# First-load order, fused low parts, single storage of rounded keys and queries, and a later fourth-pair load in an adaLN transformer block

## The chip, the cores and the metric

The kernel runs on one core of one Trainium2 chip. The metric is device microseconds of that core. TensorE (PE) does matmuls and transposes through an identity matrix, VectorE (DVE) and ScalarE (ACT) do elementwise work and read PSUM, GpSimd (POOL) does elementwise work in SBUF, and SyncE (SP) issues nearly all DMAs; in the changed kernel one DMA is issued by ACT.

## The reference

One transformer block over S = 2048 tokens of width D = 512, with 32 heads of width 16 and a hidden width F = 1792, all in float32. Six modulation vectors come from one conditioning row c.

```python
mod = (silu(c) @ w_mod)                      # c: 1 x 512, w_mod: 512 x 3072
sa, ca, ga, sb, cb, gb = six slices of 512
h = layernorm(x) * (1 + ca) + sa
q, k, v = h @ wqkv                           # 32 heads of 16
x = x + ga * (softmax(q k^T / 4) v @ wo)
h = layernorm(x) * (1 + cb) + sb
x = x + gb * (mish(h @ w1 + b1) @ w2)
```

## The kernel before

Every large product is made of three products of parts. A value is rounded to a high part (`hi_copy`) and its remainder is the low part (`lo_sub`), and high by high, high by low and low by high are summed in PSUM (`mm3`). `h_h` and `h_l` are the two parts of h, `wh` and `wl` those of a slice of wqkv, `qh` and `ql` those of the keys or queries just made.

**First stage.** Four blocks of 512 tokens (`tb` = 0 to 3), each of four tiles `xt`. For a block: row statistics on DVE (`stats_tb`, BN_STATS and BN_AGGR), the inverse square root on POOL (`ln_rs`), the normalisation on ACT (`apply_tb`), PE transposes (`tr_tb`), then per 128 channels `h_h` on ACT, `hf` on DVE (the same value unrounded) and `h_l` = `hf` - `h_h`, on DVE for the channels that `LOV[tb]` lists and on POOL for the others. `modc` holds 1 + ca and sa as columns, so nothing of h can be made before the conditioning row has gone through silu (`sil`), the products with `wma` (the two slices of w_mod), and back into columns. In block 0 DVE takes the statistics of block 1 before its first `hf`. After each block's matmuls the keys of the first eight heads (in block 0 the queries too) go to DRAM (`kscr`, `qscr`) and come back as operands with one head per 64 partitions.

**Operands of the scores.** A buffer `qa` or `ka` holds a pair of heads. `ka` has 48 rows per head (high, low, high of each of 16 dimensions), `qa` has 50 (high, high, low, and two rows for the row maximum, `mt`), so that one matmul sums all three products. Before the change `kscr` has 48 rows and `qscr` 50 rows per head, with the high parts stored twice. `load_pair` loads pair `pp` into one of five buffer pairs (`NR`).

**Steps.** From there on work is written out by hand in steps: 20 prologue steps (`PRO`) that take only the row maxima of the first heads (`max_pair`, L553 and L555) beside the remaining projections (`whole_units`), then T = 512 steps. Sixteen steps serve one group of four heads (one `n`): scores (L588), exponential (L591), product with the values (L606), and maxima for the group after next (L539, L541). `neg_max` (L562) closes the maxima of a group and PE goes on with the next group's first pair; eight steps later it needs the second pair. Each step has two hooks, numbered 2t and 2t+1, at which loads and stores are issued: `load_v` of group n at hook 32n - 11, the even pair of group n at 32(n-2) plus 2, 9 or 15, the odd pair at 32(n-1), the maxima's rows (`qa<-mt`) at 32n - 6. The fourth pair (pp = 3) of the first loads has a hook of its own. SP takes its DMAs strictly in that order, and the program gives them eight completion counters in turn, so an issue waits for the DMA eight before it.

The projection for the other query blocks and the MLP of finished blocks run inside these steps; a tail does the last block's MLP.

Of the kernel before, what the change touches and what calls it, by code (L numbers as in the profile page):

```python
# [8 lines left out]
F32 = mybir.dt.float32  # L9
# [9 lines left out]
def adaln_block(ctx: ExitStack, tc: tile.TileContext, x, wqkv, wo, w1, b1, w2, c, w_mod, out):  # L19
# [21 lines left out]
    LOV = ((1,), (), (1, 3), (1, 3))  # L41
# [10 lines left out]
    nc.scalar.preload_act_table_set("natural_log_exp_and_others")  # L52
# [4 lines left out]
    kscr = dram.tile([H, 48, S], F32, name="kscr")  # L57
    qscr = dram.tile([H, 50, S], F32, name="qscr")
# [16 lines left out]
    sel = cst.tile([P, 1], F32, name="sel")  # L75
    nc.gpsimd.memset(sel, 0.0)
    for k in range(DK):
        nc.gpsimd.memset(sel[32 * k:32 * k + 1, :], 1.0)
# [89 lines left out]
    def free_banks():  # L168
# [3 lines left out]
        for i in nc.cur_bb.bb.instructions:  # L172
            banks, names, made = set(), set(), set()
            for a in (*i.outs, *i.ins):
                v = getattr(a, "bass_ap", None)
                if v is not None and v.tensor.name != ring_t.tensor.name:
                    names.add(v.tensor.name)
                    if any(a is w for w in i.outs):
                        made.add(v.tensor.name)
# [66 lines left out]
    def qk_unit(kind, ct, tb, tag):  # L246
# [7 lines left out]
        def fin(h=None):  # L254
# [10 lines left out]
            scr, rows = (qscr, 50) if kind == 0 else (kscr, 48)  # L265

            def put():
                put_away.add((kind, ct, tb))
                o = 8 * ct * rows * S + tb * TB
                if kind == 0:  # L270
                    for r, src in enumerate((qh, qh, ql)):
                        nc.sync.dma_start(dap(scr, o + r * S, [[rows * S, 8], [3 * S, DH], [1, TB]]), src.bitcast(F32))
# [33 lines left out]
    def load_q(pp, rows=50):  # L306
# [5 lines left out]
        for s in range(2):  # L312
            nc.sync.dma_start(qt[64 * s:64 * s + rows, :], qscr[h + s, :rows, qb * TB:(qb + 1) * TB])

    def load_k(pp, tb=None):
# [3 lines left out]
        at_ = slice(0, S) if tb is None else slice(tb * TB, (tb + 1) * TB)  # L319
        assert {(1, h // 8, i) for i in (range(NB) if tb is None else (tb,))} <= put_away, (pp, put_away)  # L320
        for s in range(2):
            nc.sync.dma_start(kt[64 * s:64 * s + 48, at_], kscr[h + s, :, at_])
# [6 lines left out]
    with ExitStack() as es:  # L329
        lp = es.enter_context(tc.tile_pool(name="lp", bufs=1))  # L330
        cc = lp.tile([P, DK], F32, name="cc")
        nc.sync.dma_start(cc, c.rearrange("o (k p) -> p (o k)", p=P))
# [31 lines left out]
        nc.vector.tensor_mul(sil, cc, e)  # L364

# [21 lines left out]
        def first_norm():  # L387

            mv = lp.tile([P, 4, 2], F32, tag="ln_mv4", name="ln_mv4", bufs=2)
            rs = lp.tile([P, 4, 4], F32, tag="ln_rs4", name="ln_rs4", bufs=3)  # L390
            for h in range(2):
                two = slice(2 * h, 2 * h + 2)
                for i in range(2 * h, 2 * h + 2):
                    st_ = lp.tile([P, 6], F32, tag="ln_st", name="ln_st", bufs=4)
                    nc.vector.bn_stats(out=st_, in_=xts[i])
                    nc.vector.bn_aggr(out=mv[:, i, :], in_=st_)
                nc.gpsimd.tensor_scalar(rs[:, 0, two], mv[:, two, 1], 1.0, EPS, op0=ALU.mult, op1=ALU.add)
                nc.gpsimd.tensor_scalar(rs[:, 3, two], mv[:, two, 0], -1.0, 0.0, op0=ALU.mult, op1=ALU.add)
                nc.gpsimd.tensor_tensor(rs[:, 1, two], rs[:, 0, two], nhalf.to_broadcast([P, 2]), op=ALU.pow)
                nc.gpsimd.tensor_mul(rs[:, 2, two], rs[:, 3, two], rs[:, 1, two])  # L400
                if h == 0:
                    hi_k = split_hi(1, 0)
            return rs, hi_k

        def split_hi(kind, i, eng="p"):
# [4 lines left out]
        def split_lo(kind, i, hi):  # L410
            lo = lp.tile([P, DK, P], F32R, tag="wl", name="wl", bufs=2)
            lo_sub("p", lo, slices[kind, i], hi)
            slices[kind, i] = (hi, lo)

        def first_apply(rs, i, eng):
            xt = xts[i]
            if eng == "a":
                nc.scalar.activation(xt, xt, AF.Identity, scale=rs[:, 1, i:i + 1], bias=rs[:, 2, i:i + 1])
            else:
                nc.vector.tensor_scalar(xt, xt, rs[:, 1, i:i + 1], rs[:, 2, i:i + 1], op0=ALU.mult, op1=ALU.add)  # L420

        def first_tr():
            pts = [bank(("ring", "ms", "ring", "acc")[k]) for k in range(DK)]
            for ii in ((0,), (1,), (2, 3)):
                for k in range(DK):
                    for i in ii:
                        nc.tensor.transpose(pts[k][:, i * P:(i + 1) * P], xts[i][:, k * P:(k + 1) * P], ident)
            return pts

        def tr_tb(tb, ks=range(DK), pts=None):  # L430
            for k in ks:
# [9 lines left out]
                nc.vector.tensor_scalar(hf, pt, modc[:, 1, k:k + 1], modc[:, 0, k:k + 1], op0=ALU.mult, op1=ALU.add)  # L441
                lo_sub("v" if k in LOV[tb] else "p", h_l[:, k, s], hf, h_h[:, k, s])

        rs, hi_k = first_norm()
        pr, pm = [], bank()[:, :2 * DK].rearrange("p (i k) -> p i k", k=DK)
        for i in range(2):
            pr.append(ring())
            for k in range(DK):
                nc.tensor.matmul(pr[i][32 * k:32 * k + 32, :], sil[:, k:k + 1].to_broadcast([P, 32]), wma[i][:, k, :],
                                 start=True, stop=True)  # L450
        for i in range(2):
            row = lp.tile([P, D], F32, tag="hf", name="row", bufs=6)
            nc.scalar.copy(row, pr[i])
            for k in range(DK):
# [1095 lines left out]
```

## Time and profile before

| | |
|---|---|
| time before, median of 3 runs | 1691.66 us (1690.85 to 1695.13) |
| profiled execution, its own time | 1691.02 us |
| its span | 1689.2 us |
| PE, DVE, ACT, POOL busy | 99%, 85%, 80%, 49% of the span |
| first maxima matmul (L553) | 50.34 us |
| first score matmul (L588) | 101.88 us |
| DMA volume | 238.98 MB |

Rows of the timeline read: start us, us, engine, line, operation, output<-input, shapes, number of instructions, and in brackets the idle time of the engine before them and what ended it. An SPq row is the issuing of a DMA, not its transfer. In the rows of the windows the columns are: window, its length, then for PE, PEld (weight loads), DVE, ACT and POOL the busy time and the number of instructions, then the granted TensorE clock, the busy share of the DMA engines and GB/s.

### The profile page before, as it was taken

What the parts mean: (1) busy time and instruction counts of PE and PEld (TensorE: products, weight loads), DVE (VectorE), ACT (ScalarE), POOL (GpSimd) and SP (SyncE); (2) the same over time, 40 slices, a digit from 0 to 9 for tenths busy, and PEclk for the clock granted to TensorE, in tenths of its full rate; (3) what the DMA queues carried; (4) which work ended last, traced back from release to release, by engine and by line L of the source; (5) the groups of instructions that cost most, each with busy time, mean ns of one, the idle gap of its engine ahead of it and who ended that gap; (6) DMA issues with size and microseconds to landing.
All of it is one profiled execution on the core that took longest, in us unless ns stands there. A gap on an engine that the chain in (4) does not pass through costs nothing.

```text
span 1689.2 us, 33772 instructions
## 1 busy us (share of the span) xinstructions
PE 1667.3 (99%) x12418; PEld 921.5 (55%) x12418; DVE 1441.5 (85%) x2369; ACT 1355.1 (80%) x2612; POOL 821.1 (49%) x843
## 2 busy tenths in 40 slices
PE   7999999999999999999999999999999999999999
PEld 5755655555444455555555455555555455555687
DVE  8898888888989988888889888888889888883377
ACT  6257777777778998888888998888888998889674
POOL 7555224655313564556323564556323565555442
PEclk9999999999999999999999999999999999999999
DMA  7877556777755443434355434534354533533261
GB/s 248 269 244 199 147 150 185 218 223 216 231 142 146 110 94 98 117 88 129 84 137 152 115 77 93 139 77 127 87 144 122 130 94 77 144 107 132 75 230 63
DMA packets 115406, 238.98 MB, mean 141 GB/s; under 512 B 24928, under 2 KB 50544, under 8 KB 109288
## 3 DMA queue, kind: packets, MB, share of 16 engines
q1 hardware_dynamic: 115240, 236.82, 49.9%
q8 instruction: 98, 1.61, 0.4%
q14 instruction: 68, 0.56, 0.1%
HBM read 180.48 MB, written 51.45 MB: 137 GB/s over the span
## 4 chain that ended last, share of the span: by engine, by line
PE 91%; DVE 3%; ACT 3%; DMA 2%; POOL 1%; issue 1%; SPq 0%; ACTq 0%; DVEq 0%; POOLq 0%
PE bk L606 29%; PE ring L588 22%; PE ring L539 20%; PE bk L139 11%; PE bk L132 3%; PE ring L1219 2%; PE ring L132 2%; DVE mx L541 2%; ACT pr L591 1%; PE ring L553 0%; DMA qa<-mt 0%; DMA xt<-in_A_x 0%; PE ring L922 0%; DMA kscr<-qh 0%; PE ring L568 0%
## 5 line engine op out<-in xcount | busy, mean ns | idle before, releaser
L541 DVE TENSOR_REDUCE mx<-ring 128x1 f32<-128x512 f32 x1968 | 1223.1, 682 | 150.0 <-PE ring L539 136.4
L591 ACT ACTIVATE pr<-ring 128x512 f32<-128x512 f32 x2048 | 1078.4, 603 | 207.1 <-PE bk L139 124.7
L539 PE MATMUL ring<-ka,qa 64*128 64x512 f32 x1968 | 817.9, 429 | 1.4 <-ACT pr L591 1.1
L588 PE MATMUL ring<-qa,ka 64*128 64x512 f32 x2048 | 759.1, 402 | 3.4 <-ACT pr L591 1.9
L606 PE MATMUL bk<-pr,vg 128*32 128x512 f32 x4096 | 545.1, 604 | 0.0
L539 PEld LDWEIGHTS ring<-ka,qa 64*128 64x128 f32 x1968 | 350.5, 184 | 326.2 <-DVE mx L541 251.3
L588 PEld LDWEIGHTS ring<-qa,ka 64*128 64x128 f32 x2048 | 373.7, 184 | 194.7 <-DVE mx L541 111.4
L139 PE MATMUL bk<-h,w 64*128 64x512 f32 (+1 forms) x1080 | 278.1, 390 | 0.0
L139 PE MATMUL bk<-w,a_h 64*128 64x512 f32 x632 | 210.9, 413 | 0.0
L139 PEld LDWEIGHTS bk<-h,w 64*128 64x128 f32 x1080 | 178.5, 184 | 9.3 <-ACT pr L591 1.5
L606 PEld LDWEIGHTS bk<-pr,vg 128*32 128x32 f32 x4096 | 81.2, 108 | 135.4 <-issue 126.0
L139 PE MATMUL bk<-w,a_l 64*128 64x512 f32 x316 | 124.0, 392 | 0.0
L139 PEld LDWEIGHTS bk<-w,a_h 64*128 64x128 f32 x632 | 106.8, 184 | 4.3 <-ACT hb L800 1.0
L978 POOL TENSOR_TENSOR y<-yd,y 128x512 f32<-128x512 f32 x44 | 56.9, 1293 | 89.0 <-ACT yd L977 79.7
L812 POOL TENSOR_SCALAR qq<-ee 128x512 f32<-128x512 f32 x25 | 15.5, 619 | 169.6 <-ACT ee L806 169.6
L828 POOL TENSOR_TENSOR qq<-qq,rr 128x512 f32<-128x512 f32 x42 | 54.1, 1289 | 85.9 <-ACT rr L822 85.9
L814 POOL TENSOR_TENSOR hb<-hb,ee 128x512 f32<-128x512 f32 x42 | 54.1, 1288 | 79.6 <-DVE ee L810 77.7
L139 PE MATMUL bk<-w,o_hl 64*128 64x512 f32 x288 | 79.1, 405 | 0.0
L101 POOL TENSOR_TENSOR a_l<-hb,a_h 128x512 fp32r<-128x512 f32 x53 | 73.1, 1379 | 4.4
L98 POOL TENSOR_SCALAR qh<-qf 128x512 fp32r<-128x512 f32 x27 | 16.7, 619 | 90.8 <-ACT qf L262 69.4
L139 PEld LDWEIGHTS bk<-w,a_l 64*128 64x128 f32 x316 | 58.3, 185 | 3.4
L139 PE MATMUL bk<-h_h,wl 64*128 64x512 f32 x168 | 57.2, 420 | 0.2 <-ACT pr L591 0.2
(219 smaller groups left out, 1909.1 us busy)
## 6 DMA issues: line engine op xcount, KB each, us to landing
ka<-kscr SPq DMA_DIRECT2D x124, 384.0 KB
w<-w2scr SPq DMA_DIRECT2D x56, 512.0 KB
w<-w1scr SPq DMA_DIRECT2D x46, 512.0 KB
vg<-vscr SPq DMA_DIRECT2D x32, 552.0 KB
qa<-qscr SPq DMA_DIRECT2D x124, 100.0 KB
kscr<-qh SPq DMA_DIRECT2D x16, 512.0 KB
qscr<-qh SPq DMA_DIRECT2D x32, 256.0 KB
w2scr<-hl SPq DMA_DIRECT2D x14, 512.0 KB
```

The costliest lines, as they stand in the source:

```text
L101: (nc.gpsimd if eng == "p" else nc.vector).tensor_sub(lo, src, hi.bitcast(F32))
L132: nc.tensor.matmul(acc, l, r, start=start, stop=stop)
L139: i = nc.tensor.matmul(acc, l[64 * g:64 * g + 64], r[64 * g:64 * g + 64], start=start and not then, stop=bool(stop and then))
L539: nc.tensor.matmul(pm, qt[64 * s:64 * s + 64, qs * P:(qs + 1) * P], kt[64 * s:64 * s + 64, kb * TB:(kb + 1) * TB], start=True, stop=True)
L541: nc.vector.tensor_reduce(out=mxs[n][:, s, 4 * j + qs, kb:kb + 1], in_=pm, op=ALU.max, axis=AX.X)
L588: nc.tensor.matmul(p_, kt[64 * s:64 * s + 64, kc * P:(kc + 1) * P], qt[64 * s:64 * s + 64, :], start=True, stop=True)
L591: e = nc.scalar.activation(pr, p_, AF.Exp, scale=SCALE)
L606: nc.tensor.matmul(accs[n][32 * h:32 * h + 32, :], vgs[n][:, o:o + 32], pts.pop((t, h)), start=(kc == 0), stop=(kc == 15))
L814: (nc.vector if tail else nc.gpsimd).tensor_mul(hb, hb, ee)
L828: nc.gpsimd.tensor_mul(qq, qq, rr)
L978: nc.gpsimd.tensor_add(y[i], yd, y[i])
L1219: nc.tensor.matmul(po[i // 2][:, i % 2, :], l[:, s], w[:, r, :], start=(f == 0 and j == 0), stop=(f == FT - 1 and j == 2))
```

## The change

It has these parts.

1. SP loads the first four token tiles before the modulation slices; each slice is loaded in four parts, the second behind the first key weights. c is loaded by ACT as four rows and turned by a PE transpose; the dummy transposes `keep_busy` stand around it.
2. The products with `sil` are summed over the four parts in PSUM (`mod_sums`), and one transpose (`mod_cols`) gives the columns. Statistics come two tiles at a time (`stats_two`), also for block 1; the fourth tile is normalised on POOL.
3. The ones in `ka` are written by ACT; POOL's memsets of two `qa` and of `zer` stand behind the first tiles.
4. `h_l` is (transposed x * (1 + ca) - `h_h`) + sa: one DVE instruction that reads `h_h`, then an addition on DVE (for block 0 two channel groups in place of one) or on POOL.
5. `kscr` and `qscr` hold 32 and 34 rows per head, each part once. A store is two DMAs; a load of a pair is eight DMAs in place of four, and the repeated rows are made by the load's source pattern or a second DMA.
6. The fourth pair's load goes from hook -8 to hook -2, behind `load_v(0)`. In `free_banks` the four token blocks of `h_h` count apart.

```diff
-    LOV = ((1,), (), (1, 3), (1, 3))
+    LOV = ((2, 3), (), (1, 3), (1, 3))
...
-    kscr = dram.tile([H, 48, S], F32, name="kscr")
-    qscr = dram.tile([H, 50, S], F32, name="qscr")
+    kscr = dram.tile([H, 32, S], F32, name="kscr")
+    qscr = dram.tile([H, 34, S], F32, name="qscr")
...
-            scr, rows = (qscr, 50) if kind == 0 else (kscr, 48)
+            scr, rows = (qscr, 34) if kind == 0 else (kscr, 32)
 
             def put():
                 put_away.add((kind, ct, tb))
                 o = 8 * ct * rows * S + tb * TB
-                if kind == 0:
-                    for r, src in enumerate((qh, qh, ql)):
-                        nc.sync.dma_start(dap(scr, o + r * S, [[rows * S, 8], [3 * S, DH], [1, TB]]), src.bitcast(F32))
-                    return
-                hi = qh.bitcast(F32)
-                twice = bass.AP(tensor=hi.tensor, offset=hi.offset, ap=[list(hi.ap)[0], [0, 2], [1, TB]])
-                nc.sync.dma_start(dap(scr, o, [[3 * S, P], [2 * S, 2], [1, TB]]), twice)
-                nc.sync.dma_start(dap(scr, o + S, [[3 * S, P], [1, TB]]), ql.bitcast(F32))
+                for r, src in enumerate((qh, ql)):
+                    nc.sync.dma_start(dap(scr, o + r * S, [[rows * S, 8], [2 * S, DH], [1, TB]]), src.bitcast(F32))
...
-            nc.sync.dma_start(qt[64 * s:64 * s + rows, :], qscr[h + s, :rows, qb * TB:(qb + 1) * TB])
+            b, o = 64 * s, (h + s) * 34 * S + qb * TB
+            nc.sync.dma_start(qt[b + DH:b + rows, :], dap(qscr, o, [[S, rows - DH], [1, TB]]))
+            nc.sync.dma_start(qt[b:b + DH, :], dap(qscr, o, [[2 * S, DH], [1, TB]]))
...
-        at_ = slice(0, S) if tb is None else slice(tb * TB, (tb + 1) * TB)
+        at_, w = (slice(0, S), S) if tb is None else (slice(tb * TB, (tb + 1) * TB), TB)
...
-            nc.sync.dma_start(kt[64 * s:64 * s + 48, at_], kscr[h + s, :, at_])
+            b, o = 64 * s, (h + s) * 32 * S + at_.start
+            nc.sync.dma_start(kt[b + DH:b + 48, at_], dap(kscr, o, [[2 * S, DH], [0, 2], [1, w]]))
+            nc.sync.dma_start(kt[b:b + DH, at_], dap(kscr, o + S, [[2 * S, DH], [1, w]]))
...
-        cc = lp.tile([P, DK], F32, name="cc")
-        nc.sync.dma_start(cc, c.rearrange("o (k p) -> p (o k)", p=P))
+        crow = lp.tile([DK, P], F32, name="crow")
+        nc.scalar.dma_start(crow, c.rearrange("o (k p) -> (o k) p", p=P))
+        nc.scalar.preload_act_table_set("natural_log_exp_and_others")
...
-        wma = [lp.tile([P, DK, D], F32, name=f"wma{i}") for i in range(2)]
-        for i in range(2):
-            nc.sync.dma_start(wma[i], w_mod[:, i * D:(i + 1) * D].rearrange("(k p) m -> p k m", p=P))
+        wma = [[lp.tile([P, D], F32, name=f"wma{i}{k}") for k in range(DK)] for i in range(2)]
+
+        def load_mod(i):
+            for k in range(DK):
+                nc.sync.dma_start(wma[i][k], w_mod[k * P:(k + 1) * P, i * D:(i + 1) * D])
+
         for t in range(4):
             load_x(t)
+        load_mod(0)
         slice_load(1, 0, lp, lp)
+        load_mod(1)
         slice_load(0, 0, lp, lp)
...
-        nc.gpsimd.memset(zer, 0.0)
-        for i in range(NR):
-            nc.gpsimd.memset(qa[i].bitcast(F32), 0.0)
-        for i in range(2):
-            nc.gpsimd.memset(ka[i].bitcast(F32), 1.0)
-
+        for t in qa[:3]:
+            nc.gpsimd.memset(t.bitcast(F32), 0.0)
+
+        spare = ring()
+
+        def keep_busy(n):
+            for _ in range(n):
+                nc.tensor.transpose(spare[:, :P], ident, ident)
+
+        keep_busy(8)
+        cc = ring()[:, :DK]
+        nc.tensor.transpose(cc, crow, ident[:DK, :DK])
+        keep_busy(26)
...
+        hi_copy("a", ka[0], ones.to_broadcast([P, S]))
...
+        def first_tr(i):
+            for k in range(DK):
+                nc.tensor.transpose(pts[k][:, i * P:(i + 1) * P], xts[i][:, k * P:(k + 1) * P], ident)
+
+        def mod_sums(i, ks):
+            for k in ks:
+                for m in range(DK):
+                    nc.tensor.matmul(prs[i][32 * m:32 * m + 32, :P], sil[:, k:k + 1].to_broadcast([P, 32]),
+                                     wma[i][k][:, m * P:(m + 1) * P], start=(k == 0), stop=(k == DK - 1))
+
+        def mod_cols(i):
+            row = lp.tile([P, P], F32, name=f"row{i}")
+            nc.vector.tensor_copy(row, prs[i][:, :P])
+            nc.tensor.transpose(prs[i][:, P:2 * P], row, ident)
+            cols = prs[i][:, P:2 * P:32]
+            if i:
+                nc.vector.tensor_scalar_add(modc[:, i, :], cols, 1.0)
+            else:
+                nc.vector.tensor_copy(modc[:, i, :], cols)
...
-                nc.vector.tensor_scalar(hf, pt, modc[:, 1, k:k + 1], modc[:, 0, k:k + 1], op0=ALU.mult, op1=ALU.add)
-                lo_sub("v" if k in LOV[tb] else "p", h_l[:, k, s], hf, h_h[:, k, s])
+                nc.vector.scalar_tensor_tensor(hf, pt, modc[:, 1, k:k + 1], h_h[:, k, s].bitcast(F32), op0=ALU.mult,
+                                               op1=ALU.subtract)
+                if k in LOV[tb]:
+                    nc.vector.tensor_scalar_add(h_l[:, k, s], hf, modc[:, 0, k:k + 1])
+                else:
+                    nc.gpsimd.tensor_add(h_l[:, k, s], hf, modc[:, 0, k:k + 1].to_broadcast([P, TB]))
...
-        rs, hi_k = first_norm()
-        pr, pm = [], bank()[:, :2 * DK].rearrange("p (i k) -> p i k", k=DK)
-        for i in range(2):
-            pr.append(ring())
-            for k in range(DK):
-                nc.tensor.matmul(pr[i][32 * k:32 * k + 32, :], sil[:, k:k + 1].to_broadcast([P, 32]), wma[i][:, k, :],
-                                 start=True, stop=True)
-        for i in range(2):
-            row = lp.tile([P, D], F32, tag="hf", name="row", bufs=6)
-            nc.scalar.copy(row, pr[i])
-            for k in range(DK):
-                nc.tensor.matmul(pm[:, i, k:k + 1], row[:, k * P:(k + 1) * P], sel, start=True, stop=True)
-        for i in range(2):
-            first_apply(rs, i, "a")
-        split_lo(1, 0, hi_k)
-        hi_q = split_hi(0, 0, "a")
-        split_lo(0, 0, hi_q)
-        first_apply(rs, 2, "a")
-        first_apply(rs, 3, "v")
-        nc.vector.tensor_scalar_add(modc[:, 1, :], pm[:, 1, :], 1.0)
-        nc.vector.tensor_copy(modc[:, 0, :], pm[:, 0, :])
-        stats_tb(1)
-        tr_tb(0, pts=first_tr())
-        apply_tb(1)
+        for q in range(2):
+            stats_two(q)
+        first_apply(3, "p")
+        for t in (*(t.bitcast(F32) for t in qa[3:]), zer):
+            nc.gpsimd.memset(t, 0.0)
+        mod_sums(0, (0, 1))
+        first_apply(0)
+        first_tr(0)
+        mod_sums(0, (2,))
+        first_apply(1)
+        first_tr(1)
+        mod_sums(0, (3,))
+        first_apply(2)
+        first_tr(2)
+        first_tr(3)
+        mod_cols(0)
+        hi_k = split_hi(1, 0, "a")
+        hi_copy("a", ka[1], ones.to_broadcast([P, S]))
+        split_lo(1, 0, hi_k, "v")
+        mod_sums(1, range(DK))
+        mod_cols(1)
+        keep_busy(4)
+        hi_q = split_hi(0, 0, "p")
+        split_lo(0, 0, hi_q, "p")
+        for q in range(2, 4):
+            stats_two(q)
+        tr_tb(0, pts=pts)
+        for i in range(4, 8):
+            first_apply(i)
+            if i == 5:
+                slice_split(2, 0, eng="v")
...
-    for pp, h in ((2, -22), (3, -8)):
+    for pp, h in ((2, -22), (3, -2)):
```

On SP, at the start of the program, the order before is this (`cc` is c as a column, `wr` a slice of wqkv; a slice of w_mod is one DMA):

```order
L332 DMA cc<-in_c 128x4x1
L342 DMA wma_131<-in_w_mod 128x4x512
L342 DMA wma_132<-in_w_mod 128x4x512
L337 DMA xt<-in_A_x 128x512 x4
L234 DMA wr<-in_A_wqkv 128x4x128 x2
L337 DMA xt<-in_A_x 128x512 x4
```

and after the change:

```order
L332 DMA xt<-in_A_x 128x512 x4
L339 DMA wma_125<-in_w_mod 128x512
L339 DMA wma_126<-in_w_mod 128x512
L339 DMA wma_127<-in_w_mod 128x512
L339 DMA wma_128<-in_w_mod 128x512
L230 DMA wr<-in_A_wqkv 128x4x128
L339 DMA wma_129<-in_w_mod 128x512
L339 DMA wma_130<-in_w_mod 128x512
L339 DMA wma_131<-in_w_mod 128x512
L339 DMA wma_132<-in_w_mod 128x512
L230 DMA wr<-in_A_wqkv 128x4x128
L332 DMA xt<-in_A_x 128x512 x4
```

The first tokens stand ahead of both slices, the second slice stands behind the key weights, and the query weights and block 1 behind that.

On DVE, from the first block's low parts to block 2's statistics, before (the two `hf` that stand ahead of these rows read the first two banks):

```order
L101 TENSOR_TENSOR h_l<-hf,h_h 128x512
L441 TENSOR_SCALAR hf<-ring,modc 128x512
L441 TENSOR_SCALAR hf<-bk,modc 128x512
L374 BN_STATS ln_st<-xt 128x6
L375 BN_AGGR ln_mv_308<-ln_st 128x2
```

and after:

```order
L460 SCALAR_TENSOR_TENSOR hf<-ring,modc,h_h 128x512
L463 TENSOR_SCALAR h_l<-hf,modc 128x512
L460 SCALAR_TENSOR_TENSOR hf<-bk,modc,h_h 128x512
L463 TENSOR_SCALAR h_l<-hf,modc 128x512
L96 TENSOR_TENSOR wl<-wr,wh 128x1024
L382 BN_STATS ln_st<-xt 128x6
```

DVE has one low part more in block 0, both of them now additions, and the value weights' remainder (`wl`) moves ahead of the statistics.

On SP, at a pair's load inside the steps, before:

```order
L313 DMA qa_107<-qscr 50x512 x2
L322 DMA ka_105<-kscr 48x2048 x2
```

and after:

```order
L304 DMA qa_100<-qscr 34x512
L305 DMA qa_100<-qscr 16x512
L304 DMA qa_100<-qscr 34x512
L305 DMA qa_100<-qscr 16x512
L315 DMA ka_98<-kscr 32x1x2048
L316 DMA ka_98<-kscr 16x2048
L315 DMA ka_98<-kscr 32x1x2048
L316 DMA ka_98<-kscr 16x2048
```

The same pair takes eight issues in place of four.

More of the change, by code (lines that the diff above doesn't have):

```diff
@@ L176, in free_banks @@
                 if v is not None and v.tensor.name != ring_t.tensor.name:
-                    names.add(v.tensor.name)
+                    part = v.offset % (DK * S) // TB if v.tensor.name == h_h.tensor.name else 0
+                    names.add((v.tensor.name, part))
                     if any(a is w for w in i.outs):
-                        made.add(v.tensor.name)
+                        made.add((v.tensor.name, part))
                 elif v is not None:
@@ L385, in apply_tb, with stats_two, split_hi @@
                 nc.scalar.activation(xt, xt, AF.Identity, scale=rs[:, 1, i:i + 1], bias=rs[:, 2, i:i + 1])
[L387 to L405, printed above, removed]
+        def stats_two(q):
+            mv = lp.tile([P, 2, 2], F32, tag="ln_mv2", name="ln_mv2", bufs=2)
+            rs = lp.tile([P, 4, 2], F32, tag="ln_rs2", name="ln_rs2", bufs=4)
+            for i in range(2):
+                st_ = lp.tile([P, 6], F32, tag="ln_st", name="ln_st", bufs=4)
+                nc.vector.bn_stats(out=st_, in_=xts[2 * q + i])
+                nc.vector.bn_aggr(out=mv[:, i, :], in_=st_)
+                rss["x", 2 * q + i] = rs[:, :, i:i + 1]
+            nc.gpsimd.tensor_scalar(rs[:, 0, :], mv[:, :, 1], 1.0, EPS, op0=ALU.mult, op1=ALU.add)
+            nc.gpsimd.tensor_scalar(rs[:, 3, :], mv[:, :, 0], -1.0, 0.0, op0=ALU.mult, op1=ALU.add)
+            nc.gpsimd.tensor_tensor(rs[:, 1, :], rs[:, 0, :], nhalf.to_broadcast([P, 2]), op=ALU.pow)
+            nc.gpsimd.tensor_mul(rs[:, 2, :], rs[:, 3, :], rs[:, 1, :])
+        def split_hi(kind, i, eng):
             hi = lp.tile([P, DK, P], F32R, tag="wh", name="wh", bufs=2)
@@ L481, in adaln_block @@
                 stats_tb(tb + 2)
-            if tb == 0:
-                slice_split(2, 0, eng="v")
             parts = []
```

28 lines of the change are left out of this document (9 added, 19 removed).

## The prediction

> **What bounds the kernel now.** I read the page first: the busy times and the chain of work that ended last, by engine.
>
> ```profile
> span 1689.2 us, 33772 instructions
> PE 1667.3 (99%) x12418; PEld 921.5 (55%) x12418; DVE 1441.5 (85%) x2369; ACT 1355.1 (80%) x2612; POOL 821.1 (49%) x843
> PE 91%; DVE 3%; ACT 3%; DMA 2%; POOL 1%; issue 1%; SPq 0%; ACTq 0%; DVEq 0%; POOLq 0%
> ```
>
> PE carries 91% of the chain, and the change takes no matmul out of the steps. It can therefore only move the part that isn't PE: the wait at the start, single stalls inside the steps, and stalls that it adds. Next I read the timeline at the borders of the stages: the first maxima, the run of DVE reductions that paces the prologue, and the first score.
>
> ```profile
> 50.34 0.73 PE L553 MATMUL ring<-ka,qa 64*128 64x512 f32 x4
> 51.72 9.22 DVE L555 TENSOR_REDUCE mx<-ring 128x2 f32<-128x1024 f32 x8
> 101.88 0.49 PE L588 MATMUL ring<-qa,ka 64*128 64x512 f32 x1
> ```
>
> The first stage takes 50.3 us. The prologue from 50.34 to 101.88 takes 51.5, of which 40 reductions of 9.22 / 8 = 1.15 us are 46.1. A us gained before 50.34 is passed on whole, unless what DVE waits for in the prologue comes late. Third, the chain and the timeline of the first 20 us, with DMA by windows.
>
> ```profile
> 2.31 7.47 DMA xt<-in_A_x
> 9.79 0.70 DVE ln_st L395
> ...
> 3.41 5.33 DVE L362 TENSOR_SCALAR sil_e<-sil_e 128x4 f32<-128x4 f32 x1 [1.76 <-ACT sil_e L361]
> 16.66 0.68 DVE L374 BATCH_NORM_STATS2 ln_st<-xt 128x6 f32<-128x512 f32 x1
> 19.07 0.78 ACT L440 ACTIVATE h_h<-ring,modc 128x512 fp32r<-128x512 f32 x1 [2.93 <-PE ring L427]
> ...
> 2.00:4.00 2.00, 0.00 (x0) 0.00 (x0) 0.59 (x1) 0.20 (x1) 1.94 (x8) 1.00 0.74 146
> 4.00:9.00 5.00, 0.00 (x0) 0.00 (x0) 4.93 (x3) 0.00 (x0) 4.72 (x5) 1.00 1.05 408
> 9.00:13.00 4.00, 3.79 (x17) 0.82 (x18) 3.22 (x9) 0.67 (x2) 1.25 (x5) 1.00 1.09 383
> 20.00:40.00 20.00, 19.53 (x107) 15.52 (x106) 19.32 (x33) 18.35 (x29) 16.01 (x20) 1.00 0.57 170
> ```
>
> The reader is to see that the kernel starts on a transfer: DVE waits 7.47 us for the first tokens, which stand behind 2.10 MB of modulation slices. From 20 to 40 us DVE is busy 19.32 of 20 and PE 19.53, so what comes before 20 us sets when all later pieces of this stage happen.
>
> **The start.** The DMA moved 2 x 0.146 + 5 x 0.408 = 2.33 MB by 9.0; the first tile's last byte is number 2.36 million, which the third window's 383 GB/s reaches at 9.07, and its statistics began 0.7 later. After the change that byte is number 0.26 million, so the statistics can begin at about 4.5. The new limit is the second slice: its last byte is number 3.41 million (four tiles, slice, key weights, slice). At 383 GB/s from 9.0 that is 11.8; plus 0.7 to the first use is 12.5, less 0.7 since c no longer goes ahead as 512 single numbers: the window 2 to 4 had a DMA share of 0.74 against 1.05 but 146 GB/s against 408, and 0.74 / 1.05 x 408 = 288 would have moved 0.28 MB more, worth 0.7 us. So 11.8, between 11.1 and 12.5. Behind it stand a product, a copy, a transpose and a column, PE and DVE in turn; I put 1.3 us on them, an estimate from 0.2 to 0.5 for a short instruction (the chain row at 49.91 below has 0.50). The columns stand at 13.1, where the first `h_h` began at 19.07 and block 1's statistics, which came right behind the columns, at 16.66. As DVE is full from there on, the gain is that of DVE, 3.5 us (2.8 to 4.2), and not the 5.9 of `h_h`. The 5.33 us of the third row, a tiny operation held while POOL wrote its memsets, cost nothing before, since the tokens came later, and their move costs nothing. The ones that ACT writes into `ka` are hidden where ACT waits 2.93 us for PE.
>
> The pieces of DVE's row then change. Their durations stand here, with the last pieces ahead of 50.34:
>
> ```profile
> 19.88 0.81 DVE L441 TENSOR_SCALAR hf<-ring,modc 128x512 f32<-128x512 f32 x1
> 21.45 0.69 DVE L101 TENSOR_TENSOR h_l<-hf,h_h 128x512 fp32r<-128x512 f32 x1
> 37.09 1.67 DVE L101 TENSOR_TENSOR h_l<-hf,h_h 128x512 fp32r<-128x512 f32 x1
> 38.68 0.68 DVE L101 TENSOR_TENSOR ql<-ring,qh 128x512 fp32r<-128x512 f32 x1
> 39.41 0.54 PEld L132 LDWEIGHTS ring<-wh,h_h 128*128 128x128 f32 x4 [0.38 <-DVE ql L101]
> ...
> 46.57 0.68 DVE ql L101
> 48.72 1.15 DVE h_l L101
> 49.91 0.50 PE ring L132
> ```
>
> Block 0 gets one `h_l` more on DVE: 0.69, or 1.67 where POOL was busy on the same operands; I take 0.8, near the first, because the two now have only one tensor operand. The fused `hf` isn't in the trace. It reads PSUM and SBUF like `ql` (0.68) and scales like the old `hf` (0.81); over the twelve in this window that is a gain of 0 to 12 x 0.13 = 1.5, and I take 0.4, nearer to the old `hf`, whose scale it keeps. It must now wait for `h_h`, with `h_l` and the next statistics queued behind it; the old one too began at 19.88, when `h_h` (19.07 + 0.78) was done, so this costs nothing while ACT stays ahead. PE waits for DVE at 39.41 and at 49.91, so what DVE gains, PE gains. Start: -3.5 + 0.8 - 0.4 = -3.1 us; at worst -2.8 + 1.67 = -1.1, at best -4.2 + 0.69 - 1.5 = -5.0.
>
> **The prologue.** DVE waits there for PE:
>
> ```profile
> DVE mx L555 <- PE ring L553: 2.4, 8, 0.6
> ```
>
> The change takes no work from PE there, so I put 0, with up to half of the 2.4 as a gain for the range.
>
> **The maxima's rows.** In the steps I looked for waits on DMA, and for SP's row in front of the largest.
>
> ```profile
> PE ring L588 <- DMA qa<-mt: 1.2, 1, 1.2
> ...
> 30.41 1.35 SPq L272 DMA_DIRECT2D qscr<-qh  x2
> 368.63 1.23 SPq L272 DMA_DIRECT2D qscr<-qh  x2
> 371.83 3.34 SPq L577 DMA_DIRECT2D qa<-mt  x4
> ...
> 33.00:37.00 4.00, 4.00 (x32) 3.65 (x30) 3.56 (x8) 2.87 (x6) 3.05 (x7) 1.00 0.49 176
> 43.00:44.00 1.00, 1.00 (x8) 0.87 (x7) 0.08 (x1) 0.96 (x2) 0.00 (x0) 1.00 1.04 393
> ```
>
> `mt` is issued 3 us behind three query stores. Stores of this form, issued at 30.41, run alone in the window 33 to 37 with half of the DMA engines (share 0.49, 176 GB/s), where a key store fills them (43 to 44: 1.04, 393 GB/s). One store of 0.26 MB less is 0.26 / 0.176 = 1.5 us; it covers the stall of 1.2. I take -1.2 (0 to -1.2).
>
> **The loads of a pair.** These are the pieces that can cost. A quiet odd pair, and an even pair that stands behind stores:
>
> ```profile
> 1160.65 0.34 DVE L562 TENSOR_REDUCE mm<-mx 128x16 f32<-128x64 f32 x2
> 1171.06 0.68 SPq L313 DMA_DIRECT2D qa<-qscr  x2
> 1171.78 0.78 SPq L322 DMA_DIRECT2D ka<-kscr  x2
> 1206.51 0.35 DVE L562 TENSOR_REDUCE mm<-mx 128x16 f32<-128x64 f32 x2
> ...
> 1177.00:1178.00 1.00, 1.00 (x10) 0.17 (x4) 1.00 (x2) 0.89 (x3) 0.92 (x2) 1.00 0.15 33
> 1178.00:1179.00 1.00, 1.00 (x10) 0.83 (x12) 0.65 (x3) 0.95 (x2) 0.92 (x2) 1.00 0.00 0
> ...
> 401.78 3.07 SPq L313 DMA_DIRECT2D qa<-qscr  x2
> 404.89 1.40 SPq L322 DMA_DIRECT2D ka<-kscr  x2
> 415.00 0.34 DVE L562 TENSOR_REDUCE mm<-mx 128x16 f32<-128x64 f32 x2
> ```
>
> The odd pair's four issues end at 1172.56 and it has landed at about 1177.9, 5.3 later. A group lasts 1206.51 - 1160.65 = 45.9 us; the odd pair is used half a group after 1160.65, at 1183.6, so 5.7 us are to spare. Eight issues take 1.5 us more, the bytes to the operands are the same: hidden. The even pair's issues end at 406.29; 5.3 later is 411.6, use follows at 415.7, so 4.1 are to spare. Here four issues took 4.5 us since each waits for a counter, so four more may take 1.5 to 4.5 us, and up to 1.5 of transfer can come on top: a stall of 0 to 1.9. I take +0.8; two other even pairs are as near, for which the range has the rest.
>
> The Trainium skill says of this ("DMA: Bandwidth & Descriptors", section "Why a DMA increments its semaphore by 16 and not by 1") that a DMA is spread over the largest number of engines up to 16 that divides its two slowest dimensions. By that rule the new query load of 34 rows would use 2 engines where one of 50 used 10, which speaks against the change. The trace agrees as far as it can: the stores whose slowest dimension is 8 have the share 0.49, and the key stores over 128 rows 1.04; no row here shows 34 rows. By the rule the sum would be the second rival's, worked out below from rows.
>
> **Sum.** -3.1 - 1.2 + 0.8 = -3.5. The profiled execution took 1691.02 (span 1689.2 and 1.8 around it), so 1687.5 by its time. It lies 0.64 below the median of 1691.66, from which the forecast is 1688.2.
>
> **The rivals.** First, *more comes through*: `hf` takes 0.68, the prologue's waits shrink by 1.2, and no load is late: -5.0 - 1.2 - 1.2 = -7.4, 1684.3. For it: DVE full from 20 to 40. Against it: the price of `hf` at its best end.
>
> Second, *late at the near pairs*: a DMA of 34 rows runs on few engines. In 4 to 9 one of 16 engines moved 408 / 16 = 25 GB/s; 34 rows of 2 KB over two are 35 KB each, 1.4 us a load and 2.8 for both heads. With the issues a pair comes 1.5 + 2.8 = 4.3 later: still hidden with 5.7 to spare, but three even pairs with about 4.1 to spare, and 0 to 3 us more for issues, stall some 1.5 each. +4.5 in place of +0.8: 1691.9, no change. For it: the share of 0.49 above.
>
> Third, *little at the start*: `h_l` costs 1.67, the second slice comes at 12.5, and `mt` is late behind other transfers: -1.1 + 0.8 = -0.3, 1691.4, no change. For it: DVE, PE and ACT are all full from 20 to 40, and ACT has new work.
>
> Fourth, *slower*: each odd pair comes too late. It decides at a delay of 5.7 us. If the two-engine loads and the key loads that follow them in the same queues take 4.8 rather than 2.8, the delay is 1.5 + 4.8 = 6.3, and PE stands 0.6 us at each of 30 odd pairs, +18: 1691.66 - 3.5 + 18 = 1706.2. Against it: the chain shows no such stall now, and the quiet load has 5.7 to spare.
>
> That the change doesn't do what it says is no rival: the orders shown with the change have the moves.
>
> **How the numbers follow.** Forecast 0.50, with its own range 1685 to 1691; more 0.15; near pairs 0.12; little 0.08; slower 0.15. About 0.3% (5.1 us) is what a measurement of this kernel can tell from no change, so faster means below 1686.6: the first rival and about 0.18 of the forecast's 0.50, together 0.33. Slower above 1696.7 is the fourth with a few hundredths of the second, 0.18; the same is 0.49. The range from 1683 to 1698 leaves out the fourth and the outermost of the first, 0.2.
>
> **What would show it.** Right: the first `h_h` near 13.2 and block 1's first statistics near 13.1; the first maxima near 47.2 and the first score near 98.8; no wait of the score matmuls on `qa<-mt`; no PE wait of over 1 us at an odd pair's first maxima. Wrong: columns later than 14; the low part on DVE above 1.2 us; PE waiting for `ka` or `qa` half a group after each neg-max row, which is the fourth rival; or transfers of 34 rows that take over 3 us.

## The result and the profile after

The changed kernel takes 1711.44 us (median of 4 runs, 1708.49 to 1713.47) against 1691.26 in the same comparison: a ratio of 1.0112 (95% interval 1.0092 to 1.0132), 1.1% slower. The ratios here and below come with the comparison and need not be the quotient of two medians. The profiled execution took 1708.49, so its trace holds some 17 us of the loss. The chain of work that ended last:

```profile
PE 84%; DMA 7%; DVE 3%; ACT 2%; issue 2%; POOL 1%; SPq 1%; ACTq 0%; POOLq 0%; DVEq 0%
```

DMA had 2% of the chain before and has 7%; PE went from 91% to 84%. The stages in the timeline, with the first pieces of DVE behind the columns:

```profile
46.96 0.73 PE L581 MATMUL ring<-ka,qa 64*128 64x512 f32 x4
103.82 0.49 PE L616 MATMUL ring<-qa,ka 64*128 64x512 f32 x1
...
14.13 0.16 DVE L445 TENSOR_SCALAR modc<-ring 128x4 f32<-128x4 f32 x1 [0.42 <-PE ring L442]
14.44 0.69 DVE L401 BATCH_NORM_STATS2 ln_st<-xt 128x6 f32<-128x512 f32 x1
19.02 0.72 DVE L460 SCALAR_TENSOR_TENSOR hf<-ring,modc,h_h 128x512 f32<-128x512 f32 x1
```

The first maxima come 3.4 us earlier (46.96, before 50.34). The prologue then takes 56.9 us in place of 51.5, so the first score comes 1.9 later than before. The timeline of SP's issues shows why, first before, then after:

```profile
58.59 1.99 SPq L322 DMA_DIRECT2D ka<-kscr  x4
61.19 1.54 SPq L1458 DMA_DIRECT2D ep<-in_B_w  x3
94.67 2.98 SPq L577 DMA_DIRECT2D qa<-mt  x4
```

```profile
39.67 0.63 SPq L315 DMA_DIRECT2D ka<-kscr  x1
67.39 0.58 SPq L316 DMA_DIRECT2D ka<-kscr  x1
68.54 1.55 SPq L1486 DMA_DIRECT2D ep<-in_B_w  x3
99.76 2.77 SPq L605 DMA_DIRECT2D qa<-mt  x4
```

The last key load of the first stage ends at 60.6 before and at 68.0 after, though the stage began earlier. The weights of the MLP (`ep`), which SP takes next, are issued 7.3 us later, and the rows of the maxima (`qa<-mt`), without which no score can start, 5.1 us later. It is SP that is short here, not the DMA engines: in the window 62 to 68, where their share was 0.99 before, it is 0.42 after. The window after; then what POOL, PE and DVE make of the late weights, the first of the four rows before, the others after:

```profile
62.00:68.00 6.00, 6.00 (x45) 4.73 (x44) 5.46 (x5) 1.12 (x3) 0.00 (x0) 1.00 0.42 133
...
64.99 0.62 POOL L98 TENSOR_SCALAR ep<-ep 128x512 fp32r<-128x512 f32 x1 [6.78 <-DMA ep<-in_B_w]
71.89 0.63 POOL L93 TENSOR_SCALAR ep<-ep 128x512 fp32r<-128x512 f32 x1 [17.07 <-DMA ep<-in_B_w]
81.47 1.40 PE L127 MATMUL bk<-h_h,wl 128*128 128x512 f32 x4 [2.37 <-POOL wl L96]
84.49 2.36 DVE L583 TENSOR_REDUCE mx<-ring 128x2 f32<-128x1024 f32 x2 [3.85 <-PE ring L581]
```

POOL takes `ep` first and a projection's remainder (`wl`) behind it. PE waits 2.37 us for `wl`, the granted clock is 0.50 from 83 to 85, and DVE waits 3.85 us for PE. At the first neg-max row (`mm`) the lead of 3.4 us is gone: it stands at 92.42, before at 91.76. Behind that come stalls in the steps. The timeline of PE and its windows (columns as before: the last three are granted clock, DMA share, GB/s):

```profile
117.60 0.47 PE L567 MATMUL ring<-ka,qa 64*128 64x512 f32 x1 [1.16 <-DMA ka<-kscr]
119.42 0.46 PE L567 MATMUL ring<-ka,qa 64*128 64x512 f32 x1 [1.34 <-DMA kscr<-ql]
...
118.00:120.00 2.00, 0.66 (x5) 0.60 (x6) 0.78 (x2) 0.00 (x0) 0.00 (x0) 0.95 1.04 368
120.00:122.00 2.00, 2.00 (x14) 1.23 (x15) 1.73 (x3) 1.20 (x2) 1.36 (x1) 0.50 1.01 312
122.00:124.00 2.00, 2.00 (x13) 0.55 (x14) 0.26 (x1) 0.60 (x1) 1.84 (x3) 0.69 0.45 158
```

and 60 us later, SP, DVE and PE:

```profile
172.48 0.30 SPq L316 DMA_DIRECT2D ka<-kscr  x1
175.78 0.66 SPq L659 DMA_DIRECT2D sm<-ot  x1
179.99 0.25 DVE L669 RECIPROCAL rc<-sm 128x16 f32<-128x16 f32 x1 [2.64 <-DMA sm<-ot]
...
180.84 0.49 PE L616 MATMUL ring<-qa,ka 64*128 64x512 f32 x1 [1.98 <-DVE mx L569]
182.00:184.00 2.00, 2.00 (x14) 0.34 (x8) 0.57 (x1) 0.30 (x2) 0.00 (x0) 0.50 0.51 98
```

In the first place PE waits for the fourth pair's keys. In the second nothing waits for a pair: the last of its eight issues is held until 172.48 (SP waits 3.8 us of this for a load of modulation weights, `wm`), the small DMA `sm<-ot` behind it lands late, DVE waits 2.64 for it, and PE 1.98 for DVE. After both, the granted clock falls to 0.50 for a few us, which it never did in the steps of the kernel before. By the neg-max rows the changed kernel is 7.9 us behind at the second (144.10, before 136.16), 13.0 at the third (195.85, before 182.89), 14.5 at the seventh (382.11, before 367.63) and 17.2 at the last (1551.20, before 1533.97).

### The profile page after: what moved, and what is told of

It is laid out like the page before. It is cut to its first block, busy times and chain, and to the rows that moved or that the text cites. A ratio compares the mean times of both kernels' runs of the same rounds, so it can differ in the third digit from the quotient of the medians.

```text
span 1706.7 us, 34294 instructions
## 1 busy us (share of the span) xinstructions
PE 1677.6 (98%) x12491; PEld 927.8 (54%) x12491; DVE 1432.9 (84%) x2372; ACT 1358.8 (80%) x2612; POOL 813.8 (48%) x839
## 4 chain that ended last, share of the span: by engine, by line
PE 84%; DMA 7%; DVE 3%; ACT 2%; issue 2%; POOL 1%; SPq 1%; ACTq 0%; POOLq 0%; DVEq 0%
PE bk L634 27%; PE ring L616 21%; PE ring L567 18%; PE bk L134 10%; PE ring L1247 2%; DVE mx L569 2%; PE bk L127 2%; PE ring L127 2%; ACT pr L619 1%; DMA sm<-ot 1%; DMA wm<-in_w_mod 1%; DMA kscr<-qh 1%; DMA qa<-qscr 1%; DMA kscr<-ql 0%; DMA qa<-mt 0%
## 5 line engine op out<-in xcount | busy, mean ns | idle before, releaser
L1006 POOL TENSOR_TENSOR y<-yd,y 128x512 f32<-128x512 f32 x44 | 56.9, 1292 | 89.2 <-ACT yd L1005 84.3
L858 POOL TENSOR_TENSOR rr<-rr,qq 128x512 f32<-128x512 f32 x42 | 54.2, 1290 | 3.5
```

What stands on the lines that cost most here:

```text
L858: nc.gpsimd.tensor_mul(rr, rr, qq)
L1006: nc.gpsimd.tensor_add(y[i], yd, y[i])
```

## The experiments

The theories. One: the number of issues. SP takes twice as many DMAs per pair, and with eight counters each also waits for the DMA eight before; all that stands behind comes late. Two: the query load of 34 rows runs on few DMA engines. Three: the rearranged start, or the fourth pair's new place, upsets the queue.

**Parts 1 to 4 alone (e1).** Edit: the changed kernel with storage and hook of before; the blocks of `h_h` still count apart in `free_banks`.

> The changed kernel with the storage of the keys and queries and the fourth pair's place as before, so parts 1 to 4 alone. If the loss is all in the storage (theories one and two, below), the first maxima start at 47.0 us as in the changed kernel, the prologue takes 51.5 again in place of 56.9, and the time is 1691.3 - 3.4 = 1687.9. If the rearranged start itself upsets the queue (theory three), the time is above 1695.

Measured: 1693.23 us, ratio 1.0006 (0.9996 to 1.0016), no change, between the two outcomes expected. The first maxima start even earlier, at 46.13, and at the first neg-max row (87.50) the lead is 4.3 us, but it is nearly gone at the first score. Windows of the kernel before, which hold what I hadn't looked at:

```profile
62.00:68.00 6.00, 6.00 (x46) 5.00 (x46) 5.53 (x6) 1.09 (x4) 2.84 (x4) 1.00 0.99 296
92.00:98.00 6.00, 5.88 (x28) 3.73 (x27) 5.43 (x7) 0.85 (x2) 3.34 (x4) 1.00 0.97 274
```

From 62 to 104 us the DMA engines are full (share 0.91 to 1.08) before the change too: weights of the MLP, stores, pairs. In e1 the prologue ends when this queue has brought `qa<-mt`, not when DVE is done. That shows as a wait, and the wait as a slow clock:

```profile
100.79 0.46 PE L618 MATMUL ring<-qa,ka 64*128 64x512 f32 x1 [3.13 <-DMA qa<-mt]
105.06 0.79 PE L134 MATMUL bk<-h_h,wh 64*128 64x512 f32 x1 [0.29 <-ACT pr L621]
...
102.00:104.00 2.00, 1.09 (x6) 0.79 (x5) 1.27 (x4) 2.00 (x4) 0.23 (x1) 0.72 1.05 284
104.00:106.00 2.00, 1.71 (x7) 0.87 (x7) 1.32 (x2) 0.72 (x3) 1.66 (x2) 0.50 0.90 256
106.00:108.00 2.00, 2.00 (x11) 1.52 (x8) 1.38 (x2) 1.12 (x2) 0.00 (x0) 0.50 1.05 372
108.00:110.00 2.00, 2.00 (x10) 1.21 (x11) 1.34 (x3) 1.97 (x4) 0.30 (x1) 0.57 1.06 401
```

**Part 5 alone (e2).** Edit: the kernel before with the changed `kscr` and `qscr`.

> The kernel before with part 5 alone. Theory one (SP and its eight counters: twice as many issues per pair hold up every DMA behind them) and theory two (a load of 34 rows runs on few DMA engines and lands late) both expect the whole loss here: 1691.3 + 20 + 3.4 = about 1714, at least 1708. Theory three expects 1693 or less.

Measured: 1717.01 us, ratio 1.0150 (1.0131 to 1.0169), so +25 us. The loss is in the storage; theory three falls for most of it.

**The fourth pair back at hook -8 (e3).**

```diff
-    for pp, h in ((2, -22), (3, -2)):
+    for pp, h in ((2, -22), (3, -8)):
```

> The changed kernel with the fourth pair's load at hook -8 again, ahead of the first values' load. Theories one and two expect that the two stalls on ka of 1.2 and 1.3 us at the fourth pair go, and that what is queued behind the load in exchange comes later: 1707 to 1712. If the moved hook is the cause (theory three), the 4.7 us of the fourth and fifth step go and with them most of the loss: 1700 or less.

Measured: 1710.53 us, ratio 1.0110 (1.0095 to 1.0125), as the changed kernel. The stall changes its place only: the fourth pair is in time, and PE waits 5.58 us for `qa<-mt` behind it.

**The number of issues alone (e4).** Edit on the kernel before, with its storage:

```diff
-            nc.sync.dma_start(qt[64 * s:64 * s + rows, :], qscr[...])
+            nc.sync.dma_start(qt[64 * s + 32:64 * s + rows, :], src[32:rows])
+            nc.sync.dma_start(qt[64 * s:64 * s + 32, :], src[:32])
...
-            nc.sync.dma_start(kt[64 * s:64 * s + 48, at_], kscr[h + s, :, at_])
+            nc.sync.dma_start(kt[64 * s + DH:64 * s + 48, at_], kscr[h + s, DH:, at_])
+            nc.sync.dma_start(kt[64 * s:64 * s + DH, at_], kscr[h + s, :DH, at_])
```

> The kernel before, with the same storage, the same bytes and the same stores; each load of a head is only cut into two DMAs of 32 and 16 or 18 rows, so a pair takes eight issues in place of four and no load has 34 rows. Theory one expects most of the loss: 1703 to 1714, with the same waits on DMA in the prologue and the first group. Theory two expects 1691 to 1695, since no load runs on two engines.

Measured: 1707.43 us, ratio 1.0095 (1.0078 to 1.0112), +16 us with the same bytes. Its first score:

```profile
110.97 0.47 PE L591 MATMUL ring<-qa,ka 64*128 64x512 f32 x1 [1.31 <-DMA qa<-mt]
```

It is 9.1 us late. The issues alone cost, as theory one expects, but not all of the 25 us.

**Parts 1 to 4 and the hook (e5).** Edit: the changed kernel with the storage of before.

> Parts 1 to 4 and the fourth pair's load at hook -2, with the storage of before. The theory after the first runs: in the prologue the DMA engines are full from 62 to 104 us, the rows of the maxima (qa<-mt) are the last thing in that queue ahead of the first score, so what the start gains is lost in front of them; then PE's idle time of 3 us halves the granted clock for some 7 us, which costs 3 us more. With the fourth pair (0.98 MB, 2.7 us) behind those rows they land that much earlier, PE waits less than 1 us, the clock stays at 1.00, and T0 is about 98: 1691.4 - 3.5 = 1688. If the fourth pair then lands later than its use at the fifth step, PE waits there and the clock falls again: 1691 to 1694. The rival, that the rearranged start itself costs in the steps, expects no difference from the first run: 1693.

Measured: 1689.02 us, ratio 0.9980 (0.9971 to 0.9989): faster than before by 3.2 us, and better than both kernels. `qa<-mt` is issued at 92.31, the fourth pair at 97.73 behind it, and the first score has no wait:

```profile
47.51 0.73 PE L583 MATMUL ring<-ka,qa 64*128 64x512 f32 x4
98.97 0.50 PE L618 MATMUL ring<-qa,ka 64*128 64x512 f32 x1
```

The prologue takes 51.5 again, with the start's gain kept. The later hook of part 6, the only difference from e1, is thus what lets the start's gain through.

**The wait filled (e6).** Edit on e1: 12 transposes of the identity ahead of the first score.

> The run with parts 1 to 4 alone, with 12 transposes of the identity (their result isn't used) ahead of the first score, where PE stood idle for 3.1 us waiting for qa<-mt. If the idle time is what halves the clock, the clock stays at 1.00 from 100 to 112, the matmuls there take 0.39 to 0.50 in place of 0.62 to 0.79, the first two steps lose 3 us of their 7.4, and the time is 1693.2 - 3 = 1690. If something else slows those matmuls (the DMA traffic, PSUM, ACT), nothing changes: 1693, or up to 1 later by the transposes.

Measured: 1691.07 us, ratio 0.9998 (0.9989 to 1.0007). The profile did as expected:

```profile
97.59 1.47 PE L1549 MATMUL ring<-ident 128*128 128x128 f32 x12
103.00 0.50 PE L134 MATMUL bk<-h_h,wh 64*128 64x512 f32 x1 [0.51 <-ACT pr L621]
...
104.00:106.00 2.00, 1.77 (x14) 1.14 (x12) 2.00 (x4) 1.96 (x5) 0.00 (x0) 1.00 1.05 353
106.00:108.00 2.00, 2.00 (x19) 0.83 (x15) 2.00 (x4) 2.00 (x5) 1.64 (x2) 1.00 1.07 404
```

Clock 1.00 where e1 had 0.50, at the same DMA share: so the slow matmuls of e1 were not made by DMA traffic. In time the gain against e1 (0.0008 in the ratio, 1.4 us) is smaller than the 3 us expected, and the two intervals overlap; its size stays open. Nor is the filled wait all that differs in the two profiles: in e6 `qa<-mt` was issued 1.2 us earlier (93.08, in e1 94.27), and the clock was at 0.50 from 23 to 25, which it wasn't in e1.

**34 rows (e7).** Edit: e4 with the query load of a head cut at row 16, so into 16 and 34 rows, in place of 32 and 18. (The first stage loads 48 rows, here 16 and 32; the 34 rows start with the third pair.)

> As the fourth run (the kernel before with each load cut in two), but the query load of a head is cut into 34 and 16 rows in place of 18 and 32. If 34 rows run on two DMA engines as the rule says, each pair lands about 3 us later than in the fourth run and the loss grows from 16 to about 25 us, that of the storage alone: 1714 to 1718. If 34 rows are spread like others: 1705 to 1709.

Measured: 1742.87 us, ratio 1.0306 (1.0278 to 1.0334): 35 us more than e4, at the same number of issues and bytes. PE waits for `qa<-mt` three times, the longest in front of the first score:

```profile
118.24 0.76 PE L591 MATMUL ring<-qa,ka 64*128 64x512 f32 x1 [6.14 <-DMA qa<-mt]
```

Theory two is right as well, by more than I expected. That it loses more than the storage alone (+25) fits the stores: e7 still makes three query stores where e2 makes two, and from the sixth to the tenth neg-max row, among which query stores stand, it takes 204.0 us where e2 takes 185.1. That wasn't tried by itself.

**Keys as before (e8).** Edit: the changed kernel with the keys' storage and loads of before (in it the rows of keys and queries are in different orders, so its scores are other numbers; the work is the same).

> The changed kernel with the keys stored and loaded as before (48 rows, one DMA for a head) and only the queries in 34 rows: six issues per pair in place of eight, and in the first stage 24 in place of 40. If the number of issues in front of the prologue's transfers is the cause, most of the loss goes: 1692 to 1699. If the 34 rows are, it stays: 1706 or more.

Measured: 1696.70 us, ratio 1.0024 (1.0014 to 1.0034). Most of the loss goes with the keys' double issues, as theory one expected, though the 34 rows stay: the two don't add up. That either decides only where SP and the queue are behind already is a reading that fits, not a result.

**Which issues (e9, e10).** Edit: e4's cut only for the first two pairs, loaded in the first stage (`pp < 2`), and only for the later ones (`pp > 1`).

> The kernel before, where only the loads of the first two pairs, which SP issues block by block in the first stage, are cut in two: 20 more issues of 0.43 us ahead of the prologue's transfers, none in the steps. If these are the cause of the fourth run's loss, SP is 20 x 0.43 = 8.6 us late when it reaches the weights of the MLP at 61 us, the first score comes 8 to 9 us later, and the time is 1691.5 + 9 to 12 (with a clock that falls in the wait): 1700 to 1704. If the loads inside the steps are the cause, 1691 to 1694.

> The other half of the fourth run: only the loads of the pairs from the third on are cut in two, in the first stage nothing. If the first stage carries the loss, what is left is 16 less the 9 to 12 of the run above: 1693 to 1699, with the waits on the rows of the maxima at 343 to 395 us. If the odd pairs came late as the fourth rival of the prediction says, 1703 or more.

Measured: e9 1700.00 us, ratio 1.0052 (1.0038 to 1.0066), +8.8; e10 1700.10 us, ratio 1.0046 (1.0032 to 1.0059), +7.8, more than I expected. In e9 SP reaches the weights 10.4 us late and the first score comes 8.7 late, as 20 x 0.43 says (before, four issues at 45.48 take 1.71):

```profile
71.57 1.54 SPq L1467 DMA_DIRECT2D ep<-in_B_w  x3
110.54 0.47 PE L597 MATMUL ring<-qa,ka 64*128 64x512 f32 x1 [1.18 <-DMA qa<-mt]
```

In e10 the first score is where it was before, and the loss is in single places: 2.4 us by the second neg-max row (138.60), with the clock at 0.50 from 107 to 110, then some 4.5 between 370 and 470, in a wait on `qa<-mt` behind three query stores (1.24 before) and one of 1.80 us on keys at 421.4. The first of these waits:

```profile
384.53 0.47 PE L597 MATMUL ring<-qa,ka 64*128 64x512 f32 x1 [2.63 <-DMA qa<-mt]
```

**A wait at 20 us filled (e11).** Edit: e5 with 13 transposes of the identity in block 1's `tr_tb`.

> The run with parts 1 to 4 and the fourth pair behind the first values, with 13 transposes of the identity (not used) in the wait of PE from 20.3 to 21.5 us, behind which the granted clock fell to 0.50 from 22.4 to 26. If that idle time is what makes the clock fall, it stays at 1.00, the first maxima start at 46.2 in place of 47.5, and the time is 1689.0 - 1.3 = 1687.7. If it doesn't, 1689.0 as before.

Measured: 1688.44 us, ratio 0.9983 (0.9974 to 0.9992), e5 again. The clock stayed at 1.00 there, the first maxima came at 46.91 rather than 46.2, and in the profiled run the clock fell later instead, from 102 to 106, behind a wait of 1.05 us. My expectation of the time failed; what the drop at 22 us costs isn't shown, since another took its place.

**34 rows as 32 and 2 (e12).**

```diff
-            nc.sync.dma_start(qt[b + DH:b + rows, :], dap(qscr, o, [[S, rows - DH], [1, TB]]))
+            nc.sync.dma_start(qt[b + DH:b + 48, :], dap(qscr, o, [[S, 32], [1, TB]]))
+            if rows > 48:
+                nc.sync.dma_start(qt[b + 48:b + rows, :], dap(qscr, o + 32 * S, [[S, 2], [1, TB]]))
```

> The changed kernel with its query load of 34 rows cut into 32 and 2, so a pair takes ten issues in place of eight, and no large load has 34 rows. If 34 rows on two engines are a large part of the changed kernel's loss, as the seventh run suggests, the queue in front of the first scores gets shorter in spite of two more issues per pair, the waits at the fourth, fifth and twelfth step go, and the time is 1700 to 1706. If the issues alone count, it is slower than the changed kernel: 1712 to 1716.

Measured: 1696.53 us, ratio 1.0035 (1.0022 to 1.0047): 13 us of the changed kernel's loss go, in spite of two issues more per pair; I had expected 5 to 11. The waits at the fourth pair are gone, and the first score stands at:

```profile
102.73 0.50 PE L618 MATMUL ring<-qa,ka 64*128 64x512 f32 x1
```

By the third neg-max row e12 is 3.5 us behind the kernel before (186.41), the changed kernel 13.0.

What the 34 rows do stands in SP's waits (line, what it waited for, us in all, times, longest). The largest such row before and after:

```profile
SPq L322 <- DMA qa<-qscr: 0.9, 1, 0.9
SPq L670 <- DMA qa<-qscr: 17.1, 11, 2.8
```

Over all lines SP waits for query loads to land for 3.1 us before, 68.9 after, 0.2 in e12, 2.6 in e4 and 94.4 in e7.

So, in ratios from one step to the next: parts 1 to 4 and 6 give -0.0020 (e5, 3.4 us of 1691), the storage with loads cut into 32, 16 and 2 rows costs 0.0055 (e12 less e5, 9.3 us), the 34 rows 0.0077 (changed kernel less e12, 13.0 us, net of what e12's two more issues per pair cost). Formed so, they add up to the 0.0112 measured; from the intervals, the last two are uncertain by some 3 and 4 us. Of the 9.3, e9's 8.8 for the same extra issues of the first stage makes them the likely whole, shown in the kernel before and not by itself in the changed one. The place fits: e12's profiled execution is 6.3 us longer than e5's, and 6.1 of them stand by the second neg-max row (139.35, in e5 133.28).

## Why the prediction was wrong

- **Start, -3.1.** Right in size by luck: the first maxima moved by 3.4, but not from what I added up. The columns stood at 14.13 where I had 13.1, block 1's statistics began at 14.44, so DVE gained 2.2 there and not 3.5, and it then waited 1.11 for a tile. DVE after, with its row of 27.82 before as the second:

```profile
17.33 0.69 DVE L401 BATCH_NORM_STATS2 ln_st<-xt 128x6 f32<-128x512 f32 x1 [1.11 <-DMA xt<-in_A_x]
27.82 0.81 DVE L441 TENSOR_SCALAR hf<-ring,modc 128x512 f32<-128x512 f32 x1
27.31 0.72 DVE L460 SCALAR_TENSOR_TENSOR hf<-ring,modc,h_h 128x512 f32<-128x512 f32 x1
35.73 0.49 DVE L463 TENSOR_SCALAR h_l<-hf,modc 128x512 fp32r<-128x512 f32 x1
```

  At block 1's first `hf` only 0.5 was left. The rest came in blocks 2 and 3, where the four `h_l` on DVE took 2.6 us in all as additions and 5.2 before, a gain that my sum puts at nothing. `hf` took 0.72 to 0.75, between my ends of 0.68 and 0.81; `h_l` in block 0 0.78 and 0.49 where I took 0.8.
- **Prologue, 0.** The term failed: the prologue got 5.3 us longer. I read DVE's row and concluded that a us gained before 50.34 is passed on whole, and put no price on my own condition, that what DVE waits for comes in time. The DMA windows of that stretch, 62 to 104 us, were not looked at; the queue was as full as DVE, and in e1 `qa<-mt` at its end took the gain. In the changed kernel what came late was first of all `wl`: 4.0 of the 5.3 us are lost by the first neg-max row. With the loads of before and part 6 (e5) the gain is passed on, so what made this term fail is the next one.
- **Loads of a pair, +0.8.** The step that failed most, at its first word: I priced eight issues for the pairs inside the steps only. The first two pairs are loaded block by block, with 20 issues before and 40 after, and SP stands at each. These rows were on SP's timeline. At the 0.50 us of one issue at 58.59 (1.99 for four) 20 more make 10 us, and everything of the prologue is behind them; e9 measured 8.8 for them.
- **Maxima's rows, -1.2.** The step before 394.8 us still lasts 3.92 us after the change, 4.21 before: 0.3 of 1.2 came. With 32 and 2 rows (e12) the same step lasts 2.9, without a wait. That the smaller store pays when SP isn't behind fits this, but it wasn't tried by itself.
- **Second rival (34 rows).** The mechanism was right and its price for a quiet pair nearly so. The timeline and windows of a quiet odd pair after the change:

```profile
1187.70 0.25 SPq L304 DMA_DIRECT2D qa<-qscr  x1
...
1194.00:1195.00 1.00, 1.00 (x12) 0.48 (x6) 0.67 (x2) 0.87 (x3) 0.92 (x2) 1.00 0.29 41
1195.00:1196.00 1.00, 1.00 (x12) 0.81 (x10) 0.98 (x2) 0.96 (x3) 0.92 (x2) 1.00 0.11 41
1196.00:1197.00 1.00, 1.00 (x12) 0.24 (x9) 1.00 (x3) 1.00 (x3) 0.91 (x2) 1.00 0.10 24
```

  The pair is done about 9.2 us after its first issue, 6.8 before; I had 4.3 later, it is 2.4. The tail is carried by a share of 0.10 to 0.11, so by 1.7 of 16 engines. This agrees with the rule of the Trainium skill ("DMA: Bandwidth & Descriptors", section "Why a DMA increments its semaphore by 16 and not by 1") by which 34 rows go to 2 engines. What I had wrong was the place: I priced it for three near pairs, 1.5 us each, but it costs 13 us, since SP, which waits for a DMA's counter, stood 68.9 us for such loads.
- **Fourth rival (slower).** The sign was this one's, the mechanism not: quiet odd pairs are still in time, and a late group lasts as long as before:

```profile
1177.30 0.35 DVE L590 TENSOR_REDUCE mm<-mx 128x16 f32<-128x64 f32 x2
1223.16 0.35 DVE L590 TENSOR_REDUCE mm<-mx 128x16 f32<-128x64 f32 x2
```

  45.86 us, as before (1160.65 to 1206.51). Of the 17.2 us by which the last neg-max row is late, 13.0 stand by the third one (195.85), the rest in a few places later. I gave 0.18 to slower because I looked for the stall where a wait is tight, not where SP and the queue have no slack.

## What to carry to other kernels

When a change adds DMAs, count every issue on the queue from the first use of the changed function, also where it is called with other arguments, multiply by the time of one issue, and ask what is queued behind; here 20 issues of 0.43 us ahead of the prologue's transfers cost 8.8 us. An engine that seems to bound a stretch is only one bound: look at the DMA share of the same windows, and at the row of the engine that issues, before passing a gain on. And give a DMA a number of rows that spreads over the engines: 32 and 2 rows are better than 34, though they are one DMA more.

## What the runs showed of the hardware

A wait of PE can cost more than itself: behind it the granted clock falls to 0.50, and matmuls of 0.39 to 0.50 us take 0.62 to 0.79. From the windows above, the time at half clock was (0.05 + 0.50 + 0.31) x 2 / 0.5 = 3.4 us in the changed kernel at 120, and (0.28 + 0.50 + 0.50 + 0.43) x 2 / 0.5 = 6.8 in e1 behind a wait of 3.13. The Trainium skill ("TensorE: Matmul & The Clock Gate", section "What's actually happening") tells of half the clock after an idle window of about 3.4 us, and of windows that run freely; the half and the multiples of 3.4 agree. A whole idle window doesn't: the waits ahead of these drops, 1.20 to 3.13 us, are shorter. The length of the wait doesn't decide either: the wait of 2.63 us in e10 was followed by no drop, the changed kernel's of 1.98 by one; a wait of 1.20 us that ends at 21.5 us was followed by a drop in e5 and by none in the changed kernel. A window that runs freely would do that; that it is the window, and not what else differs there, wasn't tried.
